# Attention heads paired j with j+6 in both batches, and the first loads cut by partition halves

## The chip, the core and the metric

The kernel runs on one core of one Trainium2 chip. The time is device microseconds of a whole execution; the number that counts is the median of several executions. The kernel before took 660.87 us (three runs: 656.98, 660.87 and 662.31). The profile shown here is of one further execution that took 657.37 us.

## The reference

Two batches of 12 heads, 448 queries and keys, 64 numbers per head, all float32. The scores of the heads are mixed before the softmax by a 12 by 12 matrix, and the probabilities are mixed again after it:

```python
scores = scale * np.matmul(q, k.transpose(0, 1, 3, 2))
scores = np.einsum('bhij,hg->bgij', scores, w_pre)
attn = softmax(scores)                       # over the last axis
attn = np.einsum('bhij,hg->bgij', attn, w_post)
x = np.matmul(attn, v)
```

The result (896 rows of 768) goes through two feed-forward pairs of layers, 768 to 2048 to 768, the first with a hard-swish and the second with a leaky unit with a learned slope. Their weights are handled as 64-bit bit patterns and rebuilt as pairs of float32 numbers, a high and a low part, so that three products of the two parts give the precision.

## The kernel before, in words

**Stages.** Attention fills roughly the first 180 us of the program, the two feed-forward layers the rest. In attention the 448 queries of a batch are cut into four tiles of 120, 120, 120 and 88 queries, so there are eight tiles. For every tile the scores of 12 heads are computed as six pairs of heads (`qk`): one head of a pair lives in partitions 0 to 63 of the key tile `kst` and the query tile `qst`, the other in partitions 64 to 127. Each pair is four matrix products of 448 columns (two blocks of queries for each head; in the profile each counts as two instructions), and its two PSUM tiles are copied to the score tile `S` by ScalarE (first head) and VectorE (second head).

**From scores to mixing.** The mixing by `w_pre` needs, for ten queries, all 12 heads on the partition axis. This is made by a DMA from SBUF to SBUF (`pull`): 120 rows of 1792 bytes, issued by SyncE, two pulls for each mixing step. A step (`premix`, `exp`, `norm`, `post`) then mixes, takes the exponential, and mixes again. `S` must hold all heads of a tile before its first pull can start.

**Order.** The program is written out by hand, and each engine executes its list in order. SyncE issues nearly all DMAs; ScalarE issues a few at the very start. The completion of a DMA is counted on one of eight semaphores that are handed out in turn, so each DMA waits, before it is issued, for the one eight places earlier in the program.

**The start.** The queries of tile 0 come in three pieces (pair 0, pairs 1 and 2, pairs 3 to 5), each cut into the two partition halves: SyncE issues the lower half and ScalarE the upper half. The keys of batch 0 come in five DMAs of all 128 partitions: pair 0 (by ScalarE), pairs 1, 2 and 3 alone, and pairs 4 and 5 together. The array `k0` in memory has the even heads in its first 64 rows and the odd heads in the other 64, so that pair j is heads 2j and 2j+1. The query array has one row for each of the 64 numbers of a head, and in it, for each tile, the 12 heads one after the other; a pair of heads 2j and 2j+1 therefore takes pieces of 120 floats (480 bytes) that lie two heads apart. The queries of tile 1 come in two pieces of two halves, with the small loads of `w_pre` and `w_post` in between, and the queries of the other tiles in two halves each. All keys of batch 1 come later, in four DMAs of one partition half and three pairs each, from rows that lie two heads apart (1792-byte pieces).

The lines that the change touches are `load_k0` (L112), `load_k` (L115), `load_q` (L132), `qk` (L163) and the list of first loads (L538 to L554). The copies of `S` are at L566, the pulls at L189, the first mixing product at L199, the second one at L238.

Of the kernel before, what the change touches and what calls it, by code (L numbers as in the profile page):

```python
# [18 lines left out]
Z = 4  # L19
# [16 lines left out]
def kernel(  # L36
# [15 lines left out]
    nc = tc.nc  # L52
    _, D, H, S = k.shape
    B, D = q.shape[0], D // 2
# [13 lines left out]
    tiles = []  # L68
    groups = []
    for b in range(B):  # L70
        for i0 in range(0, S, GP):
            n = min(GP, S - i0)
            t = len(tiles)
# [33 lines left out]
    with tc.manual_schedule():  # L107
        xT = xtp.tile([128, KD, NT], F32, name="xT")
        v_t, q_st = {}, {}
        k_st = [kq.tile([128, H // 2, S], F32, tag=f"k{b}", name="kst") for b in range(B)]  # L110

        def load_k0(p, z, q=nc.sync):  # L112
            q.dma_start(out=k_st[0][:, p:z, :], in_=k0[:, p:z, :])

        def load_k(b, o, p, z):  # L115
            src = k[b - 1, D * o:D * o + D].rearrange("p (j o) s -> p j o s", o=2)
            nc.sync.dma_start(out=k_st[b][D * o:D * o + D, p:z, :], in_=src[:, p:z, o, :])

        wraw = late.tile([128, WP], F32, tag="wraw", bufs=1, name="wraw")
        nc.gpsimd.memset(wraw, 0.0)  # L120
        wpre = late.tile([128, Q], F32, tag="wpre", bufs=1, name="wpre")
        nc.gpsimd.memset(wpre, 0.0)
        wpost = late.tile([128, WP], F32, tag="wpost", bufs=1, name="wpost")
        load_k0(0, 1, nc.scalar)
        nc.vector.memset(three, 3.0)
        nc.vector.memset(warm, 0.0)
        nc.scalar.activation(out=warm, in_=warm, func=ACTF.Exp)

        def upper(n):
            return max(n - (Q - Z), 36)  # L130

        def load_q(ti, *at, qs=(nc.sync, nc.sync)):  # L132
            T = tiles[ti]
            n = T["n"]
            m = H // 2 * n
            t = q_st[ti] = kq.tile([128, Z + H // 2 * GP], F32, tag="qst", bufs=2, name="qst")
            nc.gpsimd.memset(t[:, :Z], 0.0)
            z = Q + m - n + upper(n)
            if z > Z + m:
                nc.gpsimd.memset(t[:, Z + m:z], 0.0)  # L140
            at = (0, *at, H // 2)
            for x, y in zip(at, at[1:]):
                for o in range(2):
                    d = slice(D * o, D * o + D)
                    a = T["i0"] * H
                    src = q[T["b"], d, a:a + H * n].rearrange("p (j o n) -> p j o n", o=2, n=n)
                    qs[o].dma_start(
                        out=t[d, Z + x * n:Z + y * n].rearrange("p (j n) -> p j n", n=n),
                        in_=src[:, x:y, o, :],
                    )  # L150
                yield

# [8 lines left out]
        S_t, MT = {}, {}  # L161

        def qk(ti, j, tag="sc"):  # L163
            n = tiles[ti]["n"]
            if j == 0:
                S_t[ti] = s_pool[(NTILE - 1 - ti) % 3].tile([128, H, S], F32, tag="S", name="S")
            pool_ = psB if tag == "sc" else psA
            ps = [pool_.tile([128, 512], F32, tag=tag, bufs=2, name="sc") for _ in range(2)]
            t = q_st[ti]
            k_ = k_st[tiles[ti]["b"]]  # L170
            for o in range(2):
                b = j * n
                for a, z, r in ((b, b + Q, 0), (b + Q, b + Q + upper(n), Q)):
                    nc.tensor.matmul(  # L174
                        ps[o][r:r + z - a, :S], t[D * o:D * o + D, a:z], k_[D * o:D * o + D, j, :],
                        start=True, stop=True,
                    )
            return [(S_t[ti][:Z + n, 2 * j + o, :], ps[o][:Z + n, :S]) for o in range(2)]

        d_t, mx_t, e_t, sm_t, wr_t, pt_t = {}, {}, {}, {}, {}, {}  # L180

# [292 lines left out]
        def in_chain(i, xs, c):  # L474
            p = ptile()[:, :S]
            in_part(p, i, xs, c, 0, KD)
            return p
# [57 lines left out]
            return i  # L535


        q0 = load_q(0, 1, 3, qs=(nc.sync, nc.scalar))  # L538
        next(q0)
        load_k0(1, 2)  # L540
        next(q0)
        load_k0(2, 3)
        load_k0(3, 4)
        next(q0)
        load_k0(4, H // 2)
        for c in range(2):
            a = GH * c
            nc.sync.dma_start(out=wpre[Z + GH * c:Z + GH * c + GH, :GH], in_=w_pre[a:a + GH, a:a + GH])
        q1 = load_q(1, 3)
        next(q1)  # L550
        for c in range(2):
            a = GH * c
            nc.sync.dma_start(out=wraw[Q * c:Q * c + GH], in_=w_post[a:a + GH, a:a + GH])
        next(q1)  # L554
        for _ in range(4):
            d_buf.append(late.tile([128, 2, S], F32, tag=f"pull{len(d_buf)}", bufs=1, name="pull"))
            nc.gpsimd.memset(d_buf[-1][:Z], 0.0)
# [10 lines left out]
        for j in range(H // 2):  # L568
            s_out(qk(0, j, ("sc", "mx")[j % 2]))
# [7 lines left out]
        for i in range(NC):  # L577
            a = 2 * (14 + 8 * i)
# [26 lines left out]
        for c in range(4):  # L605
            load_at.setdefault((3, 5, 7, 8)[c], []).append(lambda c=c: load_v(0, c))
            load_at.setdefault(10 + c, []).append(
                lambda c=c: load_k(1, c % 2, 3 * (c // 2), 3 * (c // 2) + 3)
            )
            load_at.setdefault(tiles[tps]['s'] // 2 + 5 + c, []).append(lambda c=c: load_v(1, c))  # L610

        for p_ in range(-2, NP + 1):
            if p_ == -2:
                for g in range(6):
                    if g == 2:
                        list(load_q(2))
                    pull(g)
# [12 lines left out]
            if 0 <= p_ < NP:  # L630
                premix(p_)
            av_add()
            two = [lambda ti=ti, j=j: qk(ti, j, "mx" if p_ < 0 and j % 2 else "sc") for ti, j in qk_at.get(p_, [])]
            pend = [f() for f in (two if p_ < 0 else two[:1])]
            if 0 <= p_ < NP:
# [46 lines left out]
        for f in range(NC):  # L682
            p = in_chain(f, x_t, 1)
# [134 lines left out]
```

## Time and profile before

| | us |
|---|---|
| median of three runs | 660.87 |
| lowest and highest | 656.98, 662.31 |
| profiled execution, whole | 657.37 |
| its span, first to last instruction | 655.5 |
| TensorE busy in the span | 635.8 (97%) |
| start of the first mixing step | 17.09 |

The span is 1.87 us shorter than the whole execution. TensorE is the busiest engine; the granted clock was 0.997 of full speed over the span. The times in the profile's rows count from the start of the span. In the rows, a wait is written behind an instruction in square brackets with the engine or DMA that seems to have ended it; `issue` means that the profile shows no such event.

### The profile page before, as it was taken

What the parts mean: (1) busy time and instruction counts of PE and PEld (TensorE: products, weight loads), DVE (VectorE), ACT (ScalarE), POOL (GpSimd) and SP (SyncE); (2) the same over time, 40 slices, a digit from 0 to 9 for tenths busy, and PEclk for the clock granted to TensorE, in tenths of its full rate; (3) what the DMA queues carried; (4) which work ended last, traced back from release to release, by engine and by line L of the source; (5) the groups of instructions that cost most, each with busy time, mean ns of one, the idle gap of its engine ahead of it and who ended that gap; (6) DMA issues with size and microseconds to landing.
All of it is one profiled execution on the core that took longest, in us unless ns stands there. A gap on an engine that the chain in (4) does not pass through costs nothing.

```text
span 655.5 us, 17580 instructions
## 1 busy us (share of the span) xinstructions
PE 635.8 (97%) x7464; PEld 558.9 (85%) x7464; DVE 407.2 (62%) x640; ACT 354.1 (54%) x664; POOL 291.5 (44%) x236
## 2 busy tenths in 40 slices
PE   7988899999899999999999999999999999999997
PEld 2666687777689999999999999999999999999997
DVE  4754575756545778787734543489999997443401
ACT  4776788887765665666444533444444444444310
POOL 2111131323533454545577545445544555777430
PEclk9999999999899999999999999999999999999999
DMA  5778654754401332233344242213322224335202
GB/s 164 241 221 196 177 143 171 212 182 128 131 3 50 101 137 100 96 108 132 98 145 144 97 145 96 97 54 110 125 98 96 97 96 138 136 136 206 97 0 85
DMA packets 34923, 81.82 MB, mean 125 GB/s; under 512 B 11420, under 2 KB 24988, under 8 KB 34844
## 3 DMA queue, kind: packets, MB, share of 16 engines
q1 hardware_dynamic: 34268, 80.27, 37.9%
q8 instruction: 59, 0.97, 0.6%
q10 hardware_dynamic: 576, 0.41, 0.2%
q14 instruction: 20, 0.16, 0.1%
HBM read 58.65 MB, written 2.75 MB: 94 GB/s over the span
## 4 chain that ended last, share of the span: by engine, by line
PE 87%; issue 5%; POOL 4%; ACT 1%; DVE 1%; DMA 0%; POOLq 0%; DVEq 0%; ACTq 0%
PE p L466 63%; PE pt L238 6%; PE av L301 6%; PE mx L199 6%; PE sc L174 6%; POOL wb L388 2%; POOL wlo L399 2%; ACT e L214 1%; DVE nm L205 1%; DMA qst<-in_q_dram 0%; ACT MT L253 0%; ACT xh L461 0%; DVE xT L279 0%; POOL wr L226 0%; DVE o L737 0%
## 5 line engine op out<-in xcount | busy, mean ns | idle before, releaser
L399 POOL TENSOR_TENSOR wlo<-wb,whi 128x768 fp32r<-128x768 f32 x64 | 126.8, 1981 | 130.7 <-ACT whi L393 130.7
L388 POOL TENSOR_TENSOR wb<-wb,wst 128x768 int32<-128x768 int32 x64 | 125.4, 1960 | 81.6 <-DVE wb L381 64.9
L466 PE MATMUL p<-xh,whi 128*128 128x448 f32 x384 | 140.6, 366 | 0.0
L466 PE MATMUL p<-xh,wlo 128*128 128x448 f32 x384 | 139.6, 364 | 0.0
L466 PE MATMUL p<-gh,whi 128*128 128x448 f32 x384 | 139.3, 363 | 0.0
L466 PE MATMUL p<-gh,wlo 128*128 128x448 f32 x384 | 138.9, 362 | 0.1
L466 PE MATMUL p<-gl,whi 128*128 128x448 f32 x384 | 138.7, 361 | 0.0
L466 PE MATMUL p<-xl,whi 128*128 128x448 f32 x384 | 138.7, 361 | 0.0
L373 DVE TENSOR_SCALAR wb<-wb 128x768 f32<-128x768 f32 x64 | 52.1, 814 | 81.6 <-ACT wb L357 81.6
L357 ACT ACTIVATE wb<-wst 128x768 f32<-128x768 f32 x64 | 58.3, 912 | 69.7 <-DMA wst<-in_w_out_dram 53.6
L393 ACT CAST whi<-wb 128x768 fp32r<-128x768 f32 x64 | 53.2, 832 | 48.4 <-PE p L466 30.1
L205 DVE TENSOR_REDUCE nm<-mx 128x1 f32<-128x448 f32 x90 | 52.4, 619 | 42.7 <-PE mx L199 40.5
L238 PEld LDWEIGHTS pt<-wr,e 60*64 60x64 f32 (+1 forms) x2880 | 60.1, 134 | 20.9 <-issue 11.8
L466 PEld LDWEIGHTS p<-xh,wlo 128*128 128x128 f32 x384 | 72.4, 188 | 5.6
L466 PEld LDWEIGHTS p<-gh,wlo 128*128 128x128 f32 x384 | 72.0, 187 | 5.9 <-POOL wlo L399 0.4
L466 PEld LDWEIGHTS p<-xl,whi 128*128 128x128 f32 x384 | 72.1, 188 | 5.0
L466 PEld LDWEIGHTS p<-xh,whi 128*128 128x128 f32 x384 | 72.3, 188 | 4.4 <-issue 0.2
L466 PEld LDWEIGHTS p<-gh,whi 128*128 128x128 f32 x384 | 72.1, 188 | 4.5
L214 ACT ACTIVATE e<-mx,nm 128x448 f32<-128x448 f32 x90 | 56.7, 640 | 35.3 <-DVE nm L205 34.8
L466 PEld LDWEIGHTS p<-gl,whi 128*128 128x128 f32 x384 | 71.9, 187 | 4.4
L226 POOL TENSOR_SCALAR wr<-wpost,sm 128x60 f32<-128x60 f32 x74 | 25.3, 356 | 113.2 <-DVE sm L222 110.9
L381 DVE SCALAR_TENSOR_TENSOR wb<-wst,wb 128x768 uint32<-128x768 uint32 x64 | 67.5, 1055 | 1.1
(50 smaller groups left out, 799.1 us busy)
## 6 DMA issues: line engine op xcount, KB each, us to landing
wst<-in_w_out_dram SPq DMA_DIRECT2D x32, 768.0 KB
wst<-in_w_in_dram SPq DMA_DIRECT2D x27, 768.0 KB
pull<-S SPq DMA_DIRECT2D x88, 210.0 KB
wst<-in_w_in_dram SPq DMA_DIRECT2D x10, 384.0 KB
v<-in_v_dram SPq DMA_DIRECT2D x16, 168.0 KB
out_dram<-o SPq DMA_DIRECT2D x12, 224.0 KB
qst<-in_q_dram SPq DMA_DIRECT2D x8, 180.0 KB
kst<-in_k_dram SPq DMA_DIRECT2D x4, 336.0 KB
```

The costliest lines, as they stand in the source:

```text
L174: nc.tensor.matmul(ps[o][r:r + z - a, :S], t[D * o:D * o + D, a:z], k_[D * o:D * o + D, j, :], start=True, stop=True,)
L199: nc.tensor.matmul(ms[r][Q * c:Q * c + Q, :S], wpre[a:z], d[a:z, c, :], start=True, stop=True)
L205: nc.vector.tensor_reduce(nm, m[:, :S], axis=AX.X, op=ALU.max, negate=True)
L214: nc.scalar.activation(out=e, in_=ms[o][:, :S], func=ACTF.Exp, bias=nms[o], accum_out=sm[:, o:o + 1])
L238: nc.tensor.matmul(ts[c][Q * z:Q * z + m, u:u + GH], e[a:a + GH, j:j + m], wr[a:a + GH], start=True, stop=True,)
L357: nc.scalar.activation(t, s[:, :, 1].bitcast(F32), ACTF.Abs)
L373: nc.vector.tensor_scalar(t, t, W_MAX, W_MIN, ALU.min, ALU.max)
L381: nc.vector.scalar_tensor_tensor(u, st_t[i][:, :, 1], 0xC0000000, u, ALU.bitwise_and, ALU.bitwise_or)
L388: nc.gpsimd.tensor_tensor(n, n, st_t.pop(i)[:, :, 0].bitcast(I32), ALU.add)
L393: nc.scalar.copy(hi, b_t[i])
L399: nc.gpsimd.tensor_tensor(lo, b_t.pop(i), w_t[i][0].bitcast(F32), ALU.subtract)
L466: nc.tensor.matmul(p, wt[a], xt[c], start=(first and z == 0), stop=(last and z == 2))
```

## The change

Heads are now paired j with j+6, in both batches, so that the lower partition half holds heads 0 to 5 and the upper half heads 6 to 11. The pieces of a partition half then lie side by side in memory. The queries of a tile come as rows of 6 times 120 floats, 2880 bytes (2112 for the tiles of 88), one DMA for each partition half; for tile 0 the three pieces are given up. The keys of batch 1 come from rows of three heads side by side (5376 bytes). The array `k0` keeps its layout in memory (even heads in the first 64 rows), so the keys of batch 0 are loaded for each partition half apart: its first three slots get even heads and its last three odd heads. That gives the order of pairs 0 2 4 1 3 5 in batch 0, and eight DMAs of 64 partitions instead of five of 128. The scores land at the same place in `S` as before.

```diff
-        def load_k0(p, z, q=nc.sync):
-            q.dma_start(out=k_st[0][:, p:z, :], in_=k0[:, p:z, :])
+        def load_k0(m, p, z, q=nc.sync):
+            o, a = p // 3, 3 * m + p % 3
+            q.dma_start(
+                out=k_st[0][D * m:D * m + D, p:z, :], in_=k0[D * o:D * o + D, a:a + z - p, :]
+            )
 
         def load_k(b, o, p, z):
-            src = k[b - 1, D * o:D * o + D].rearrange("p (j o) s -> p j o s", o=2)
-            nc.sync.dma_start(out=k_st[b][D * o:D * o + D, p:z, :], in_=src[:, p:z, o, :])
+            a = o * (H // 2)
+            nc.sync.dma_start(
+                out=k_st[b][D * o:D * o + D, p:z, :], in_=k[b - 1, D * o:D * o + D, a + p:a + z, :]
+            )
...
-        load_k0(0, 1, nc.scalar)
+        load_k0(0, 0, 1)
+        load_k0(1, 0, 1, nc.scalar)
...
-                    a = T["i0"] * H
-                    src = q[T["b"], d, a:a + H * n].rearrange("p (j o n) -> p j o n", o=2, n=n)
+                    a = T["i0"] * H + o * m
                     qs[o].dma_start(
-                        out=t[d, Z + x * n:Z + y * n].rearrange("p (j n) -> p j n", n=n),
-                        in_=src[:, x:y, o, :],
+                        out=t[d, Z + x * n:Z + y * n], in_=q[T["b"], d, a + x * n:a + y * n]
                     )
...
+            h0 = j if tiles[ti]["b"] else (0, 2, 4, 1, 3, 5)[j]
             for o in range(2):
-                b = j * n
+                b = h0 * n
...
-            return [(S_t[ti][:Z + n, 2 * j + o, :], ps[o][:Z + n, :S]) for o in range(2)]
+            return [(S_t[ti][:Z + n, h0 + o * (H // 2), :], ps[o][:Z + n, :S]) for o in range(2)]
...
-        q0 = load_q(0, 1, 3, qs=(nc.sync, nc.scalar))
-        next(q0)
-        load_k0(1, 2)
-        next(q0)
-        load_k0(2, 3)
-        load_k0(3, 4)
-        next(q0)
-        load_k0(4, H // 2)
+        list(load_q(0, qs=(nc.sync, nc.scalar)))
+        load_k0(0, 1, 3)
+        load_k0(1, 1, 3, nc.scalar)
+        for p, z in ((3, 4), (4, 6)):
+            for m in range(2):
+                load_k0(m, p, z)
+        list(load_q(1))
         for c in range(2):
...
-        q1 = load_q(1, 3)
-        next(q1)
...
-        next(q1)
```

The DMAs that SyncE issues from the start of the program to the first two pulls were these (`qst` are queries, `kst` keys, with partitions x floats; `wpre` and `wraw` the mixing matrices):

```order
L147 DMA qst<-in_q_dram 64x120
L113 DMA kst<-in_k_dram 128x448
L147 DMA qst<-in_q_dram 64x2x120
L113 DMA kst<-in_k_dram 128x448 x2
L147 DMA qst<-in_q_dram 64x3x120
L113 DMA kst<-in_k_dram 128x896
L548 DMA wpre<-in_w_pre_dram 60x60 x2
L147 DMA qst<-in_q_dram 64x3x120 x2
L553 DMA wraw<-in_w_post_dram 60x60 x2
L147 DMA qst<-in_q_dram 64x3x120 x2
L189 DMA pull<-S 120x1x448 x2
```

And they are now, in the same stretch:

```order
L114 DMA kst<-in_k_dram 64x448
L152 DMA qst<-in_q_dram 64x720
L114 DMA kst<-in_k_dram 64x896
L114 DMA kst<-in_k_dram 64x448 x2
L114 DMA kst<-in_k_dram 64x896 x2
L152 DMA qst<-in_q_dram 64x720 x2
L552 DMA wpre<-in_w_pre_dram 60x60 x2
L555 DMA wraw<-in_w_post_dram 60x60 x2
L194 DMA pull<-S 120x1x448 x2
```

Fifteen DMAs ahead of the pulls have become thirteen. The queries of tile 1 stand now ahead of `wpre`, in two DMAs where there were four, and the keys of pairs 3 to 5 are four DMAs of half the partitions where there were two of all.

ScalarE's list at the same place was:

```order
L113 DMA kst<-in_k_dram 128x448
L127 ACT_TABLE_LOAD
L127 ACTIVATE warm<-warm 128x16
L147 DMA qst<-in_q_dram 64x120
L147 DMA qst<-in_q_dram 64x2x120
L147 DMA qst<-in_q_dram 64x3x120
L566 COPY S<-sc 124x448 x12
```

And is now:

```order
L114 DMA kst<-in_k_dram 64x448
L133 ACT_TABLE_LOAD
L133 ACTIVATE warm<-warm 128x16
L152 DMA qst<-in_q_dram 64x720
L114 DMA kst<-in_k_dram 64x896
L567 COPY S<-sc 124x448 x12
```

ScalarE issues the upper half of the queries in one DMA where it issued three, and the upper half of the keys of the first three pairs.

## Rows read from the trace of the kernel before

**Rows 1.** The page, first part: busy time, share of the span, instructions.

```profile
PE 635.8 (97%) x7464; PEld 558.9 (85%) x7464; DVE 407.2 (62%) x640; ACT 354.1 (54%) x664; POOL 291.5 (44%) x236
```

**Rows 2.** Stretches: length, engines' busy time (instructions), granted clock, DMA share, GB/s.

```profile
0.00:16.50 16.50, 12.89 (x96) 4.87 (x96) 6.90 (x13) 7.40 (x14) 4.26 (x15) 1.00 0.60 165
16.50:30.00 13.50, 13.26 (x272) 7.72 (x273) 9.61 (x24) 10.04 (x27) 2.40 (x10) 1.00 0.74 245
30.00:60.00 30.00, 26.42 (x802) 18.84 (x795) 17.35 (x42) 22.91 (x61) 4.92 (x18) 1.00 0.79 213
...
180.00:600.00 420.00, 419.95 (x2511) 391.51 (x2504) 289.44 (x367) 208.65 (x314) 228.31 (x120) 1.00 0.32 109
```

**Rows 3.** Timeline of TensorE's weight loads: start, length, instruction, idle time before.

```profile
3.58 0.31 PEld L174 LDWEIGHTS sc<-kst,qst 64*64 64x64 f32 x4 [3.58 <-issue]
...
5.80 0.33 PEld L174 LDWEIGHTS sc<-kst,qst 64*64 64x64 f32 x8 [1.22 <-DMA kst<-in_k_dram]
...
8.72 0.43 PEld L174 LDWEIGHTS sc<-kst,qst 64*64 64x64 f32 x8 [1.10 <-ACT S L566]
9.70 0.34 PEld L174 LDWEIGHTS sc<-kst,qst 64*64 64x64 f32 x8 [0.54 <-ACT S L566]
10.63 0.34 PEld L174 LDWEIGHTS sc<-kst,qst 64*64 64x64 f32 x8 [0.59 <-ACT S L566]
...
15.87 0.19 PEld L174 LDWEIGHTS sc<-kst,qst 64*64 64x64 f32 x4 [0.25 <-DVE S L566]
17.05 0.22 PEld L199 LDWEIGHTS mx<-pull,wpre 64*64 64x64 f32 x4 [0.99 <-issue]
```

**Rows 4.** Timeline of VectorE: the copy that ends tile 0's scores.

```profile
11.80 1.38 DVE L566 COPY S<-sc 124x448 f32<-124x448 f32 x2 [0.31 <-PE sc L174]
```

**Rows 5.** Timeline of SyncE's DMA issues in the first 27 us.

```profile
5.37 0.34 SPq L113 DMA_DIRECT2D kst<-in_k_dram  x1
...
12.49 1.79 SPq L189 DMA_DIRECT2D pull<-S  x2
14.40 1.34 SPq L147 DMA_DIRECT2D qst<-in_q_dram  x2
15.78 10.25 SPq L189 DMA_DIRECT2D pull<-S  x12
```

**Rows 6.** DMA issues by size, from the page: one slot of keys.

```profile
kst<-in_k_dram ACTq DMA_DIRECT2D x1, 224.0 KB
```

**Rows 7.** Stretches of particular transfers, columns as in the second group.

```profile
2.00:9.00 7.00, 5.39 (x28) 1.81 (x32) 1.25 (x2) 1.72 (x4) 2.15 (x3) 1.00 0.90 253
...
8.50:9.00 0.50, 0.50 (x8) 0.28 (x8) 0.00 (x0) 0.00 (x0) 0.00 (x0) 1.00 1.01 332
11.00:13.00 2.00, 2.00 (x24) 0.72 (x16) 1.55 (x3) 1.40 (x3) 0.41 (x2) 1.00 0.42 92
...
50.50:51.00 0.50, 0.50 (x8) 0.15 (x4) 0.47 (x1) 0.00 (x0) 0.00 (x0) 1.00 1.07 190
```

**Rows 8.** Timeline of weight loads at the second mixing step.

```profile
20.35 0.20 PEld L199 LDWEIGHTS mx<-pull,wpre 64*64 64x64 f32 x6 [0.61 <-DMA pull<-S]
```

**Rows 9.** Chain of work that ended last: its longest stalls in attention.

```profile
46.58 1.39 issue
...
69.73 1.33 issue
...
75.50 1.24 issue
...
119.93 1.29 issue
```

**Rows 10.** SyncE's issues of later queries: three of them.

```profile
44.19 1.75 SPq L147 DMA_DIRECT2D qst<-in_q_dram  x2
...
94.17 1.35 SPq L147 DMA_DIRECT2D qst<-in_q_dram  x2
...
116.69 1.34 SPq L147 DMA_DIRECT2D qst<-in_q_dram  x2
```

## The prediction

> **What bounds the kernel now.** I read the page's busy times first: TensorE is busy for 635.8 of 655.5 us [rows 1], so what can be won lies in its idle stretches. The table by stretches then shows where these are. From 180 to 600 us there are none (419.95 of 420 us), and no line of that part is touched. In attention there are some: 3.6 us between 30 and 60 us, and the first 16.5 us, where TensorE is called busy for 12.89 us but runs only 96 products [rows 2]. The weight loads tell more there than the products, whose ends are modelled. Pair 0 of tile 0 starts at 3.58 us, pair 1 at 5.80 after 1.22 us of waiting for keys, pair 3 at 8.72, pair 4 at 9.70 and pair 5 at 10.63 [rows 3]. The waits before 8.72 and 9.70 are put down to copies of S; those copies had been done, so I take them for DMA waits, of queries and of the last keys. From pair 5 of tile 0 to the last of tile 1 (15.87) six pairs take 5.24 us, 0.87 us each: the pace of the copies out of PSUM.
>
> What hangs on this start: tile 0's last copy is the first of the two VectorE copies from 11.80 us, so it ends at about 12.49 [rows 4], and there SyncE issues the first pull [rows 5]. The two pulls are issued by 14.28, and the first mixing step loads its weights at 17.05 [rows 3], 2.8 us behind. The next two pulls, at 0.85 us each in the row of twelve from 15.78 [rows 5], are issued by 17.49, and the second step waits for a pull until 20.35 [rows 8], 2.86 us behind. So the first steps stand in the shadow of the pulls, and these in that of tile 0's scores. From there on TensorE is busy, 13.26 of 13.5 us up to 30 us [rows 2]. A start that comes d earlier moves the end by d.
>
> **The change part by part.** *Bytes of tile 0.* Six slots of keys at 224 KB [rows 6] are 1.376 MB, and 128 rows of 2880 bytes of queries 0.369 MB, together 1.745 MB, the same before and after. Before, 2 to 9 us moved 7 times 253 GB/s, 1.77 MB [rows 7], so the last keys were in at about 9.0, and pair 4, which needs them, loaded its weights 0.7 us later. Pair 5 follows 0.93 us behind, and the first pull 2.79 us behind pair 4.
>
> *What pieces of 480 bytes cost.* The second half of tile 1's queries, in such pieces and alone on the queue, moved 2 times 92 GB/s, 0.184 MB, in 0.42 times 2 us of engine time, 219 GB/s when busy; the last keys, in all 128 partitions, ran at 332 GB/s [rows 7]. With rows of 2880 bytes I expect the queries to cost what keys cost, 0.57 us less of DMA time for a tile (0.369 MB at 219 against 332 GB/s). The three pieces of tile 0's queries also no longer stand among the keys of pairs 1 to 5.
>
> *What halves cost.* The trace has one clean look at a load of one partition half: the keys of batch 1, between 50.5 and 51 us, at 190 GB/s with the DMA engines busy throughout (share 1.07) [rows 7]. That is the lower bound for the new loads; 332 GB/s is the upper. The first 1.057 MB (queries and three slots of keys) have their lower half on SyncE's queue and their upper half on ScalarE's, both in flight: I take 310 GB/s, near the upper bound, 3.4 us. The other three slots, 0.688 MB, follow on SyncE's queue alone, half after half: I take the middle, 261 GB/s, 2.6 us. From 2.0 us that ends at 8.0, so pair 4 comes at 8.7, **1.0 us earlier**. At 332 GB/s throughout it ends at 7.3 (1.7 us earlier), at 190 at 11.2 (2.2 us later).
>
> The trace's 190 GB/s for one half has a rule beside it. The Trainium skill, SBUF — State Buffer, section "Door 1: The DMA port swizzle", says that DMA bandwidth goes by how many of the 16 ports the partitions reach, and that partitions 0 to 63 reach eight. By it the last three slots would run at half of 332, an estimate of 166 GB/s, and take 4.1 us, and pair 4 would come 0.5 us later than before instead of 1.0 earlier. The trace's one look agrees with the direction of the rule.
>
> *Pair 0 waits for more.* It needs now all queries and one slot of keys, 0.598 MB, at 310 GB/s until 3.9, so it starts near 4.6 instead of 3.58. With pairs 0.87 us apart, pair 4 could start at 8.1; the keys at 8.7 are later, so this costs nothing. Were the keys faster, it would cap the gain at 1.6 us.
>
> *Tile 1.* Its queries stand behind the keys on SyncE's queue, now in two DMAs: 0.369 MB at 261 GB/s, in by 9.4, usable at 10.1. Tile 1's first pair follows pair 5 (9.6) at 10.5. Cover of 0.4 us; without it the pulls would still start on time, only TensorE's last pairs before the first mixing step would slip. `wpre` and `wraw` come behind these queries; the first mixing step at 16 us is far off.
>
> *SyncE's later issues.* Tile 2's queries are issued from 14.40 for 1.34 us in a row of DMAs without a gap [rows 5], and the second step waits behind them. Below, they might cost 0.34 us each, as the cheapest key DMA does [rows 5], a gain of 0.66 us; above, nothing changes. The two loads still spread over 64 partitions as before, so I take 0. All later queries and the keys of batch 1 become shorter transfers that no instruction of TensorE is shown to wait for: 0. ScalarE issues one DMA fewer before its first copy at 5.4 us: hidden, 0.
>
> **Sum:** 657.37 us of the profiled execution less 1.0 is 656.4. That execution lies 3.5 us below the median of the three runs; less 1.0 from there is 659.9. Since a new median can fall at either, I forecast the middle, **658.0 us**.
>
> **Rivals.** *The halves win, and the start gets later.* On SyncE's queue each half is written before the other, and two loads follow in the same order; if that holds the whole of the first load near 190 GB/s, pair 4 comes up to 2.2 us later and the time is 659.6 on the profile's base, slower than before. It decides at 249 GB/s on average, where the last byte is in at 9.0 as before. For it: the 190 GB/s of one half. Against it: two halves on two queues for 60% of the bytes. Chance 17%.
>
> *The long stalls go too.* The chain has stalls of 1.39, 1.33 and 1.29 us at 46.58, 69.73 and 119.93 [rows 9] with no releaser in the profile, the first and the third 2.4 and 3.2 us behind the start of an issue of queries [rows 10]. If crowding by 480-byte pieces makes such stalls, I would have all three go: 4.0 us more, 652.4. Against it: a stall of 1.24 us at 75.50 has no such load beside it, and the load at 94.17 no such stall [rows 9, 10]. Chance 12%.
>
> *The start is shifted and nothing comes of it*: the keys arrive at the old time, since SyncE must still issue seven loads for them and tile 0's queries one after the other, as before, at 0.34 us or more each [rows 5]. Then 657.4 on the profile's base. Chance 14%.
>
> **How the numbers follow.** Forecast 57%, rivals 17, 12 and 14. About 1% is what a measurement of this kernel can tell from no change: 6.6 us, and its own runs spread over 5.3. The bounds of the likeliest case are 1.7 us of gain under the lowest run (655.3) and 0.3 under the highest (662); the second rival reaches down to 652.4, the first up to 664.5 from the highest run. I take **653.5 to 662**, which leaves about half of each rival outside. Faster by over 1% needs the second rival and a low run, or stalls gone that I do not see: 10%. Slower by over 1% needs the first rival at its worst and a high run: 4%. Within 1%: 86%.
>
> **What would show it.** In the profile after, the weight loads of tile 0: pair 0 near 4.6 us, pair 4 near 8.7 and pair 5 near 9.6, the first pull near 11.5, the first mixing step near 16.1. The DMA rate between 2 and 8 us should be near 290 GB/s; below 249 the first rival is right. If pair 4 is at 8.7 and the mixing step still at 17, the chain from scores to pulls is not what I say. If the stalls by the query loads have gone, the second rival is. I should be wrong altogether if the feed-forward part changed its length, since nothing there is touched.

## The result and the profile after

The changed kernel took 663.0 us (median of 20 executions, 657.47 to 669.57) against 659.89 us for the kernel before beside it (20 executions, 652.69 to 664.95): a ratio of **1.0051**, 95% interval 1.0027 to 1.0076. It is slower by half a per cent, where the forecast was 658.0 us and a range of 653.5 to 662. The profiled execution took 658.5 us, span 656.7, granted clock 0.996. The ratios in this document compare fast executions only (none over 1.5% above the fastest of its kernel) and are therefore not the quotients of the medians; the differences at equal clock below use all executions and change by 0.2 us at most without the slow ones.

First the timeline of TensorE's weight loads in the changed kernel (start, length, instruction, idle time before), the answer to [rows 3, 8].

```profile
6.77 0.44 PEld L179 LDWEIGHTS sc<-kst,qst 64*64 64x64 f32 x8 [6.77 <-issue]
8.03 0.68 PEld L179 LDWEIGHTS sc<-kst,qst 64*64 64x64 f32 x8 [0.82 <-DMA kst<-in_k_dram]
9.18 0.41 PEld L179 LDWEIGHTS sc<-kst,qst 64*64 64x64 f32 x4 [0.47 <-ACT S L567]
...
10.67 0.41 PEld L179 LDWEIGHTS sc<-kst,qst 64*64 64x64 f32 x8 [0.52 <-ACT S L567]
11.48 0.35 PEld L179 LDWEIGHTS sc<-kst,qst 64*64 64x64 f32 x8 [0.40 <-ACT S L567]
...
18.70 0.22 PEld L204 LDWEIGHTS mx<-pull,wpre 64*64 64x64 f32 x4 [0.83 <-issue]
...
21.83 0.22 PEld L204 LDWEIGHTS mx<-pull,wpre 64*64 64x64 f32 x6 [0.47 <-DMA pull<-S]
```

Pair 0 starts at 6.77 us (before 3.58, forecast 4.6) and pair 4 at 11.48 (before 9.70, forecast 8.7). The first mixing step is at 18.70 (before 17.05, forecast 16.1). It is 1.65 us late, and the second step still 1.48.

The chain of waits (start, length, what) says what pair 0 waited for. In the changed kernel:

```profile
0.74 0.59 SPq L114
...
1.38 5.29 DMA qst<-in_q_dram
...
6.80 11.84 PE sc L179 x94
...
198.72 302.42 PE p L471 x1511
```

The same view of the kernel before:

```profile
0.74 2.73 DMA qst<-in_q_dram
...
3.61 13.23 PE sc L174 x90
...
197.91 302.42 PE p L466 x1511
```

The queries are issued at 1.38 us and counted as landed 5.29 us later; before, the small first piece was there after 2.73 us. The lower lines are the longest unbroken run of feed-forward products: 302.42 us in both, so that part kept its length, as the prediction said it must. It starts 0.81 us later, so in these two executions about half of the 1.65 us at the first step is left there.

Two more views of the changed kernel: SyncE's queue (start, length, what), the answer to [rows 5],

```profile
0.74 0.59 SPq L114 DMA_DIRECT2D kst<-in_k_dram  x1
1.38 0.82 SPq L152 DMA_DIRECT2D qst<-in_q_dram  x1
2.25 3.17 SPq L114 DMA_DIRECT2D kst<-in_k_dram  x5
...
14.30 1.80 SPq L194 DMA_DIRECT2D pull<-S  x2
```

and the stretches, columns as in [rows 2, 7]:

```profile
2.00:4.50 2.50, 0.00 (x0) 0.00 (x0) 0.00 (x0) 0.82 (x2) 2.15 (x3) 1.00 0.87 220
4.50:9.00 4.50, 2.19 (x12) 1.02 (x16) 0.27 (x1) 0.41 (x1) 0.00 (x0) 1.00 1.01 287
2.00:9.00 7.00, 2.19 (x12) 1.02 (x16) 0.27 (x1) 1.23 (x3) 2.15 (x3) 1.00 0.96 263
16.50:30.00 13.50, 13.42 (x278) 7.35 (x273) 10.08 (x22) 9.74 (x25) 1.89 (x8) 1.00 0.69 247
30.00:60.00 30.00, 27.15 (x791) 20.23 (x786) 16.82 (x41) 22.11 (x58) 4.85 (x17) 0.94 0.69 208
```

The first pull is issued 2.82 us behind pair 4 and the first mixing step 4.40 us behind the first pull, near the forecast's 2.8 and 4.6. So the chain from scores to pulls is as described; its start is late. From 2 to 9 us the DMA engines moved 263 GB/s, more than before (253) and above the 249 at which the first rival decides. Its first 2.5 us had only 220 GB/s, where 310 was forecast; the kernel before had 226 there. From 16.5 to 30 us TensorE is busy 13.42 of 13.5 us (13.26 before), so nothing there takes the late start back. From 30 to 60 us it is busy longer than before (27.15 against 26.42) for fewer products, at a granted clock of 0.94 instead of 1.00. The kernel before has such a stretch too, 0.94 between 150 and 180 us, so this need not be the change's doing (see the last section).

Last, the score products of the changed kernel by duration (count; minimum, median, maximum in ns; first and last start), the long ones first and then the short ones, without the few of a length between:

```profile
L179 PE MATMUL sc<-kst,qst x16: 947/951/999, 6.8 to 9.2; 64*64 64x448 f32 x8, 64*60 64x448 f32 x8
...
L179 PE MATMUL sc<-kst,qst x58: 536/537/588, 10.3 to 16.0; 64*64 64x448 f32 x29, 64*60 64x448 f32 x29
```

The same of the kernel before:

```profile
L174 PE MATMUL sc<-kst,qst x24: 947/951/1006, 3.6 to 8.1; 64*64 64x448 f32 x12, 64*60 64x448 f32 x12
...
L174 PE MATMUL sc<-kst,qst x66: 536/537/587, 9.5 to 15.9; 64*64 64x448 f32 x33, 64*60 64x448 f32 x33
```

One and the same product takes 951 ns at first and 537 later. The kernel before passes to the short products at 9.5 us, the changed one at 10.3. Before, half of tile 0's 48 products were long, while the keys were still coming; now a third are, but all of them fall behind the arrival of the queries. The prediction saw none of this: it took 0.87 us a pair throughout.

### The profile page after: what moved, and what is told of

Read it like the earlier page. It is cut to its first block, busy times and chain, and to the rows that moved or that the text cites. A ratio compares the mean times of both kernels' runs of the same rounds, so it can differ in the third digit from the quotient of the medians.

```text
span 656.7 us, 17575 instructions
## 1 busy us (share of the span) xinstructions
PE 633.6 (96%) x7464; PEld 557.2 (85%) x7464; DVE 412.5 (63%) x640; ACT 355.0 (54%) x664; POOL 290.3 (44%) x236
## 4 chain that ended last, share of the span: by engine, by line
PE 86%; issue 5%; POOL 4%; ACT 2%; DVE 1%; DMA 1%; SPq 0%; POOLq 0%; ACTq 0%; DVEq 0%
PE p L471 63%; PE pt L243 6%; PE av L306 6%; PE mx L204 6%; PE sc L179 5%; POOL wb L393 2%; POOL wlo L404 2%; ACT e L219 1%; DMA qst<-in_q_dram 1%; DVE nm L210 1%; ACT MT L258 0%; DVE xT L284 0%; POOL wr L231 0%; ACT S L567 0%; ACT wst L368 0%
## 5 line engine op out<-in xcount | busy, mean ns | idle before, releaser
L404 POOL TENSOR_TENSOR wlo<-wb,whi 128x768 fp32r<-128x768 f32 x64 | 125.2, 1956 | 129.3 <-ACT whi L398 129.3
L243 PEld LDWEIGHTS pt<-wr,e 60*64 60x64 f32 (+1 forms) x2880 | 59.0, 134 | 24.3 <-issue 15.8
L386 DVE SCALAR_TENSOR_TENSOR wb<-wst,wb 128x768 uint32<-128x768 uint32 x64 | 72.4, 1130 | 1.1
```

What stands on the lines that cost most here:

```text
L243: nc.tensor.matmul(ts[c][Q * z:Q * z + m, u:u + GH], e[a:a + GH, j:j + m], wr[a:a + GH], start=True, stop=True,)
L386: nc.vector.scalar_tensor_tensor(u, st_t[i][:, :, 1], 0xC0000000, u, ALU.bitwise_and, ALU.bitwise_or)
L404: nc.gpsimd.tensor_tensor(lo, b_t.pop(i), w_t[i][0].bitcast(F32), ALU.subtract)
```

## The experiments

**How the times compare.** The executions of any kernel here spread over some 10 us, and the mean granted clock of an execution (0.987 to 1.000) goes with its time and explains about half of the spread. A line fitted through the 98 executions of the kernel before and 33 of the changed one, gathered over all comparisons, has a slope of -620 us per unit of clock, 0.6 us for each 0.001. "At equal clock" below is the difference to those 98 after this correction, with its standard error; the printed ratio has no such correction. The slow first products are not part of that clock (see the last section), so the correction leaves them in.

**When a load is in.** The trace also keeps when each of the 16 DMA engines reported its share of a load. The times of "the last engine" below are read from there; the first instruction that waits for a load starts right behind its last engine (pair 0 of the changed kernel at 6.77 us, 0.10 behind the last report of its queries).

**e1: the queries uncut, nothing else.** The kernel before, with tile 0's queries as one load of two halves (still in 480-byte pieces):

```diff
-        q0 = load_q(0, 1, 3, qs=(nc.sync, nc.scalar))
-        next(q0)
+        list(load_q(0, qs=(nc.sync, nc.scalar)))
...
```

> The kernel before with one edit: the queries of tile 0 come in one DMA for each partition half (six 480-byte pieces a row) instead of three pieces. Theory 1 (pair 0 now waits for all queries of tile 0, and that is what delays the start): pair 0's weight load moves from 3.58 us to 5.0 or later, the first mixing step from 17.05 to 17.8 to 18.7, and the time is 0.5 to 1.7 us longer. Theory 2 (the key loads of one partition half are what delays it): all loads of keys are of 128 partitions here, so pairs 1 to 5 and the first mixing step stay where they were (within 0.3 us of 17.05) although pair 0 starts later.

Measured: 664.12 against 660.23 us, ratio 1.0055 (1.0018 to 1.0093); at equal clock +2.9 ± 0.6 us. Weight loads of this kernel:

```profile
4.59 0.30 PEld L174 LDWEIGHTS sc<-kst,qst 64*64 64x64 f32 x4 [4.59 <-POOL pull L554]
7.75 0.30 PEld L174 LDWEIGHTS sc<-kst,qst 64*64 64x64 f32 x8 [2.85 <-DMA qst<-in_q_dram]
...
20.15 0.19 PEld L199 LDWEIGHTS mx<-pull,wpre 64*64 64x64 f32 x2 [0.55 <-issue]
```

The second half of pair 0 waits 2.85 us for queries, and the mixing step is 3.1 us later than before: the direction of theory 1, but well beyond its 17.8 to 18.7 us and its 0.5 to 1.7 us of time. Giving up the pieces is alone enough to make the kernel slower, and with 480-byte pieces it costs more than in the changed kernel.

**e2: the keys whole.** The changed kernel, with the keys of batch 0 laid out in memory by heads 0 to 5 and 6 to 11, so that they come in five DMAs of 128 partitions and the order of pairs is 0 to 5 again:

```diff
+        def load_k0(p, z, q=nc.sync):
+            q.dma_start(out=k_st[0][:, p:z, :], in_=k0[:, p:z, :])
...
-            h0 = j if tiles[ti]["b"] else (0, 2, 4, 1, 3, 5)[j]
+            h0 = j
...
```

> The changed kernel with the keys of batch 0 in 128 partitions again, in five DMAs (one slot, 1, 1, 1, 2) as before: the key array is laid out with heads 0 to 5 in its first 64 rows, so the pairs come in the order 0 to 5. Queries still whole, in 2880-byte rows. Theory 1 (waiting for all queries of tile 0): pair 0 still starts at 6.0 us or later and the first mixing step stays at 18.2 or later. Theory 2 (halves of keys): pair 0 starts at 4.6 to 5.2 and the first mixing step comes at 16.5 or earlier.

Measured: 659.59 us, ratio 0.9988 (0.9963 to 1.0013); at equal clock -0.8 ± 0.4 us. Weight loads:

```profile
4.54 0.31 PEld L175 LDWEIGHTS sc<-kst,qst 64*64 64x64 f32 x4 [4.54 <-POOL pull L553]
5.59 1.03 PEld L175 LDWEIGHTS sc<-kst,qst 64*64 64x64 f32 x10 [0.75 <-DMA qst<-in_q_dram]
...
17.84 0.22 PEld L200 LDWEIGHTS mx<-pull,wpre 64*64 64x64 f32 x4 [0.66 <-issue]
```

and the stretch from 2 to 9 us:

```profile
2.00:9.00 7.00, 4.43 (x22) 2.38 (x26) 0.73 (x2) 1.71 (x4) 2.15 (x3) 1.00 1.00 302
```

Here 302 GB/s and a pair 0 at 4.54: about what the prediction assumed for the changed kernel. And yet the mixing step is at 17.84, not near 16. Neither theory's numbers hold as written: the start is earlier than the one said, the step later than the other said. Something beyond the arrival sets the step. Nor is the shape of the keys' loads all that differs: SyncE now issues its half of the queries first, at 0.74 us instead of 1.38, so 0.64 of the 2.2 us that pair 0 gains on the changed kernel may be that.

**e3: the pairing alone.** e2 with tile 0's queries in the old three pieces and tile 1's in the old two:

```diff
-        list(load_q(0, qs=(nc.sync, nc.scalar)))
+        q0 = load_q(0, 1, 3, qs=(nc.sync, nc.scalar))
+        next(q0)
...
```

> As the run with keys of 128 partitions, and the queries of tiles 0 and 1 cut into the pieces that they had before, in the order of before: so the kernel before with heads paired j with j+6 and all pieces of a row side by side, and nothing else. Both theories: pair 0 starts near 3.6 us again. If rows without gaps help as I forecast, the keys of pairs 4 and 5 come earlier (0.5 us or so, since queries no longer take 219 GB/s), the first mixing step at 16.2 to 16.8, and the time is 0.3 to 1 us shorter than before; if the rest of the changed kernel's loss lies in the later loads of queries and of batch 1's keys, the time is 1 us or more longer than before although the start is early.

Measured: 659.76 us, ratio 0.9988 (0.9953 to 1.0022); at equal clock -2.1 ± 0.5 us, the largest gain of all kernels by this measure, which its ratio does not show apart from no change. Weight loads:

```profile
3.65 0.31 PEld L175 LDWEIGHTS sc<-kst,qst 64*64 64x64 f32 x4 [3.65 <-issue]
...
6.42 0.33 PEld L175 LDWEIGHTS sc<-kst,qst 64*64 64x64 f32 x8 [1.66 <-DMA kst<-in_k_dram]
...
18.01 0.22 PEld L200 LDWEIGHTS mx<-pull,wpre 64*64 64x64 f32 x4 [0.99 <-issue]
```

The step at 18.01 misses the 16.2 to 16.8 expected. Pair 1 starts only at 6.42 us. The row puts its wait down to keys, but the last engine reported these at 5.46 us and the queries of pairs 1 and 2 at 6.32, so it waited for queries. The short products begin at 10.8 us.

**e4: the changed kernel with a first piece of queries for pair 0.**

```diff
-        list(load_q(0, qs=(nc.sync, nc.scalar)))
+        list(load_q(0, 1, qs=(nc.sync, nc.scalar)))
```

> The changed kernel with the queries of tile 0 in two pieces (pair 0 alone, then the other five) in place of one; keys in halves as in the change. Theory 1: pair 0 starts at 4.0 to 4.6 us instead of 6.77, pair 1 still waits for its queries and keys until 7.5 to 8.3, and since the copies of pair 0 are then long done the later pairs follow at 0.85 us each: first mixing step at 17.2 to 18.0 instead of 18.70. Theory 2 (the keys' halves set the pace): the first mixing step stays at 18.4 or later.

Measured: 661.11 us, ratio 1.0004 (0.9974 to 1.0034). Weight loads:

```profile
4.88 0.44 PEld L179 LDWEIGHTS sc<-kst,qst 64*64 64x64 f32 x8 [4.88 <-POOL pull L558]
7.99 0.47 PEld L179 LDWEIGHTS sc<-kst,qst 64*64 64x64 f32 x8 [2.66 <-issue]
8.79 0.41 PEld L179 LDWEIGHTS sc<-kst,qst 64*64 64x64 f32 x4 [0.33 <-issue]
...
10.39 0.43 PEld L179 LDWEIGHTS sc<-kst,qst 64*64 64x64 f32 x4 [0.44 <-ACT S L567]
...
11.88 0.43 PEld L179 LDWEIGHTS sc<-kst,qst 64*64 64x64 f32 x4 [0.44 <-ACT S L567]
...
20.35 0.22 PEld L204 LDWEIGHTS mx<-pull,wpre 64*64 64x64 f32 x4 [1.10 <-issue]
```

and its products between 9 and 14 us:

```profile
L179 PE MATMUL sc<-kst,qst x33: 537/951/999, 8.0 to 14.0; 64*60 64x448 f32 x17, 64*64 64x448 f32 x16
```

Pair 0 comes 1.9 us earlier than in the changed kernel, and the mixing step 1.65 us later, at 20.35 where 17.2 to 18.0 was expected. After pair 0 TensorE stood 2.66 us; the short products began only at 13.9 us, and the pairs from 8.79 on stand 1.5 us apart instead of 0.87. An early pair followed by a gap bought nothing. This miss made the pace of the products the next thing to test.

**r_e4, r_before, r_after: second profiles of the same kernels.**

> The changed kernel with the first pair's queries in a piece of their own, a second profile. Its first profile had pair 0 at 4.88 us, long products until 14 us and the first mixing step at 20.35, later than the changed kernel's own, while its measured time was no longer than that of the kernel before. If the gap of 2.7 us between pairs 0 and 1 keeps TensorE slow, the long products last until 12 us or later again and the mixing step comes at 19 us or later; if that profile was a stray one, the mixing step comes at 17.2 to 18.5.

> The kernel before once more, for a second profile of it. If the first mixing step of one profile is worth comparing, it comes at 17.05 us within 0.4 us here too; if the landing of the first loads or the length of the first products differs from run to run, it can lie up to 2 us away.

> The changed kernel once more, for a second profile. Theory 1 (pair 0 waits for all queries and three DMAs' worth of keys): its weight load comes again at 6.0 to 7.5 us, against 3.6 before, and the first mixing step at 18.3 to 20.5. If that first profile was a stray one: pair 0 near 4.6.

Measured: r_e4 has pair 1 at 7.88 behind a gap of 2.36 us, short products from 13.9 us on and the step at 20.34, so e4's profile was no stray. r_before has the step at 17.63, a little outside the 0.4 us expected, and r_after at 19.29: 1.66 us apart, beside 1.65 in the first two profiles.

**w_before, w_after, w_e2: TensorE kept at work before pair 0.** Products of a zeroed piece of `S`, 224 columns each, in a PSUM tile that nothing else uses at that time: three ahead of pair 0 and one ahead of pair 1 in the kernel before, seven ahead of pair 0 in the changed one, five in e2.

```diff
+        S_t[0] = s_pool[(NTILE - 1) % 3].tile([128, H, S], F32, tag="S", name="S")
+        nc.vector.memset(S_t[0][:, H - 1, :224], 0.0)
...
+        dummy = psA.tile([128, 512], F32, tag="pt", bufs=2, name="dummy")
+
+        def busy(n):
+            for _ in range(n):
+                nc.tensor.matmul(dummy[:, :224], S_t[0][:, H - 1, :128], S_t[0][:, H - 1, :224], start=True, stop=True)
...
+            busy((5, 0)[j] if j < 2 else 0)
```

> The kernel before with four products of zeros on TensorE (128 x 224), three ahead of pair 0 and one ahead of pair 1; their results are not used. In the profile before, the products of the first pairs took 951 ns each until about 8.1 us and 537 ns after that. Theory A (they are long because TensorE had been idle): the long ones end 1.5 to 2.5 us earlier, the first mixing step comes at 15.8 to 16.8, and the time falls by 0.3 to 1.2 us. Theory B (they are long because of where their data comes from, or the queue behind them): they stay long until 8 us and the first mixing step stays near 17.05 or comes later by up to 1 us.

> The changed kernel with seven such products of zeros ahead of pair 0, which waits for its data until 6.77 us anyway. Theory A: the products of tile 0 take 537 ns from pair 0 on, pairs 1 to 5 follow at 0.85 us from 8.0, the first mixing step comes at 17.0 to 17.8 instead of 18.70, and the time falls by 0.9 to 1.7 us against the changed kernel, which leaves it 0.2 to 0.4% above the kernel before. Theory B: no change in the first mixing step (18.4 or later).

> Heads paired j with j+6, keys of batch 0 in five DMAs of 128 partitions, queries in whole rows of 2880 bytes, and five products of zeros ahead of pair 0: the version that the runs so far point to. If the start is set by the landing of the loads once TensorE is warm: pair 0 at 4.6 to 5.8 us as without the zeros, products of 537 ns from pair 0 or 1 on, the later pairs at 0.8 us, pair 4 near 8.8, first mixing step at 15.8 to 16.6 against 17.84 without the zeros, and the time 0.2 to 0.5% below the kernel before. If the first mixing step is held by something else (pulls, queries of tile 1): 17 us or later, and no gain over the run without zeros.

Measured for w_after: 659.76 us, ratio 0.9982 (0.9951 to 1.0013); at equal clock 0.0 ± 0.5 us. Weight loads:

```profile
6.28 0.22 PEld L181 LDWEIGHTS sc<-kst,qst 64*64 64x64 f32 x8 [0.28 <-issue]
7.57 0.20 PEld L181 LDWEIGHTS sc<-kst,qst 64*64 64x64 f32 x8 [1.08 <-DMA kst<-in_k_dram]
...
9.93 0.34 PEld L181 LDWEIGHTS sc<-kst,qst 64*64 64x64 f32 x8 [0.41 <-ACT S L569]
...
17.20 0.19 PEld L206 LDWEIGHTS mx<-pull,wpre 64*64 64x64 f32 x2 [0.90 <-issue]
18.84 0.30 PEld L206 LDWEIGHTS mx<-pull,wpre 64*64 64x64 f32 x6 [1.46 <-DMA pull<-S]
```

and its products up to 9 us:

```profile
L181 PE MATMUL sc<-kst,qst x24: 536/536/587, 6.3 to 8.8; 64*64 64x448 f32 x12, 64*60 64x448 f32 x12
```

With work ahead of them the score products take 536 ns from the first. From pair 0 to pair 4 it is now 3.65 us instead of 4.71, and the step comes at 17.20 instead of 18.70. Of these 1.5 us some 0.5 are pair 0's own earlier start, which varies as much from one execution of the changed kernel to another (below). Beside r2_after, whose pair 0 starts alike (6.21) and whose step is at 18.25, 1.05 us remain for the pace.

w_before: 658.74 us, ratio 0.9974 (0.9938 to 1.0010), step at 17.48 where 15.8 to 16.8 was expected. Its products are short from 5.2 us on, but pairs 3 and 4 load at 8.54 and 10.25, after 1.32 and 1.37 us of waiting; the last engines reported pair 3's queries at 8.48 and pair 4's keys at 10.15. So in the kernel before, the loads hid the slow products almost wholly, and short ones are worth little there.

w_e2: 658.34 against 661.22 us, ratio **0.9948** (0.9912 to 0.9984); at equal clock -1.6 ± 0.7 us. Weight loads:

```profile
5.21 0.29 PEld L177 LDWEIGHTS sc<-kst,qst 64*64 64x64 f32 x4 [0.54 <-issue]
...
9.35 0.26 PEld L177 LDWEIGHTS sc<-kst,qst 64*64 64x64 f32 x8 [0.69 <-ACT S L564]
...
16.57 0.22 PEld L202 LDWEIGHTS mx<-pull,wpre 64*64 64x64 f32 x4 [1.11 <-issue]
```

This is the earliest first mixing step of all kernels, 1.27 us ahead of e2 and as expected, and the only kernel whose interval lies below 1: by this one comparison of twelve executions it beats the kernel before, and its median is lower than either of the changed kernel's two (663.0 and 661.38), which come from other comparisons.

**d_late: the new pairing in batch 1 only.** The kernel before, with the new `load_k`, `load_q` and `qk` where `T["b"]` is 1.

> The kernel before with the new pairing in batch 1 alone: the keys of batch 1 in 5376-byte pieces and the queries of its four tiles in 2880-byte rows (2112 for the small one), batch 0 and all first loads as before. If the changed kernel's loss lies in its start alone: the ratio is 1.000 within 0.0025. If part of it lies in the later loads: a ratio of 1.002 or more, 1.3 us, which is about what the start's 1.65 us leave unexplained of the changed kernel's 0.51%.

Measured: 660.54 us, ratio 0.9988 (0.9953 to 1.0023); at equal clock +0.1 ± 0.4 us. The shorter transfers of batch 1 cost nothing, and no gain of them can be told. This profile also has the start of the kernel before with short products from 7.4 us on instead of 9.5, and its first mixing step is at 17.27: there again the earlier short products gain nothing, and pair 4 (10.04) follows its keys (9.94).

**x_keys_sp: the upper keys of pairs 1 and 2 on SyncE.** The changed kernel with these keys issued by SyncE instead of ScalarE, so that they no longer run beside the queries on ScalarE's queue:

```diff
-        load_k0(1, 1, 3, nc.scalar)
+        load_k0(1, 1, 3)
```

> The changed kernel with the upper half of the keys of pairs 1 and 2 issued by SyncE, behind the lower half, instead of ScalarE: nothing but queries then follows the first keys on ScalarE's queue. If the queries of tile 0 land late because those keys run beside them on the other queue: pair 0 starts at 5.3 to 6.1 us instead of 6.77 to 6.90. If it is the queries' own transfer that is slow: 6.5 us or later as before.

Measured (one execution): 661.37 us; the stretch from 2 to 4.5 us has 249 GB/s, and pair 0, at 6.32, lies within what the changed kernel itself gave (6.21 to 6.90 in three profiles). That the keys crowd the queries out is not shown by pair 0. The trace shows it in part: fourteen of the 16 DMA engines reported the upper half of the queries by 4.75 us (5.44, 5.75 and 5.55 in the changed kernel), but the last one, which decides, at 5.98 (6.22, 6.51 and 5.86).

**r2_after: the changed kernel timed again.**

> The changed kernel once more, timed beside the kernel before, with the granted clock of every execution on both sides. If the start's 1.65 us is all that the change costs: at equal granted clock (0.6 us for each 0.001, from the slope of its first 20 executions) it is 1.2 to 2.1 us slower than before, and what is left of the first 0.51% is a lower mean clock in that set. If the change costs more than its start: 2.8 us or more at equal clock.

Measured: 661.38 against 660.67 us, ratio 1.0029 (0.9996 to 1.0063); the profile has pair 0 at 6.21 and the step at 18.25. Over all executions with a listed clock the changed kernel's mean is 662.46 us (33) and that of the kernel before 660.99 (98), 1.5 us apart; at equal clock 1.1 ± 0.4 us. So the change costs about 0.2%, near the shift at the first mixing step, and the first comparison's 0.5% lies above that. What is left fits the spread between sets of executions: the kernel before had 659.89 us there, 660.23 to 661.52 in the four later comparisons.

## Why the prediction was wrong

**The step that failed** is "*Pair 0 waits for more*", with its conclusion that "the keys at 8.7 are later, so this costs nothing". With it failed the term that brought the last keys in at 8.0 us. Three numbers were wrong.

*When pair 0 starts.* The prediction worked out the arrival as bytes by rate, 0.598 MB at 310 GB/s. From 2 to 4.5 us the rate was 220 GB/s, and the queries were counted as landed at 6.67 us, 5.29 us after the issue, when at 266 GB/s from 2 us on over 1.2 MB had come in. So queries and first keys did not come first: the loads issued behind them came in beside them. Fourteen of the 16 DMA engines had reported the lower half of the queries by 5.78 us, the last did at 6.67; by then fourteen had reported the upper keys of pairs 1 and 2 as well, which were issued 0.6 us later. A load counted as landed here with its slowest engine, which a sum of bytes by rate leaves out. The row that could have warned was the kernel before's own: its first piece took 2.73 us, though small. e1 shows the same without any change to the keys' halves (second half of pair 0 at 7.75).

*When the last keys are in.* The sum had 8.0 us; the last engine reported them at 10.10, and at 9.59 in the kernel before, where the prediction had 9.0. In other executions it was 10.49 and 10.10 in the changed kernel and 10.30 in the kernel before, so the halves brought the keys no earlier, and the 1.0 us of the sum was not there to be won. With whole keys (e2) it was 8.83.

*How fast the pairs follow.* The 0.87 us came from rows between 10.63 and 15.87 us. While the products take 951 ns, a pair takes 1.5 us. From pair 0 to pair 4 the changed kernel takes 4.71 us where 3.5 stood in the sum, and 3.65 with the zero products ahead (w_after). By the sum's own arithmetic, 6.77 plus 3.5 gives 10.25 for pair 4; two of the pairs at 1.5 us make it 11.5, and 11.48 was measured. Pair 1's key wait of 0.82 us adds nothing: its weights are loaded while the products of pair 0 still run, and its own products start at 8.32 us, in the step of about 0.75 us that all the long ones keep. In the prediction the keys set pair 4; in the run pair 4 followed the pairs ahead of it, 1.4 us behind its keys. Rows with 951 ns were in the trace of before, and the prediction set them aside because the ends of products are modelled. Their starts say the same: 5.83, 7.35 and 8.84 us for pairs 1 to 3 of the kernel before.

**Readings of single rows.** The waits before 8.72 and 9.70 us in the kernel before were for queries and keys, as the prediction took them: the last engines reported at 8.66 and 9.59. Pair 1's wait until 5.80 was for queries (5.70), not for keys (5.35), though the row names these.

**What held.** From pair 4 to the first pull 2.82 us (2.8), from there to the mixing step 4.40 (4.6), and the feed-forward part untouched. The time stayed within 1%, to which the prediction gave 86%, but not for the reason given: the start it had 1.0 us earlier came 1.65 us later. The later loads cost nothing (d_late). Tile 1's queries stop no pair ahead of the pulls.

**"A start that comes d earlier moves the end by d"** holds only roughly: +1.65 us at the step is 1.1 ± 0.4 at the end, and e1's +3.1 is 2.9 ± 0.6, but e4's +3.3 is 1.0 ± 0.6, and e3, whose step is 0.4 to 1.0 late, is 2.1 faster. What makes up for it in e3 and e4 stays open. Both have batch 0's queries of the later tiles in long rows, but so has the changed kernel.

**The rivals.** *The halves win* had the right sign, but not the mechanism: it decides at 249 GB/s and 263 were moved, and pair 4, 1.8 us later than before, did not wait for its keys. In part it was right all the same: with whole keys (e2) the same stretch has 302 GB/s and pair 0 comes 2.2 us earlier, though up to 0.64 us of that is the earlier issue of the queries. The rule set beside it, from the Trainium skill, SBUF — State Buffer, section "Door 1: The DMA port swizzle", would have given 166 GB/s for the last three slots; from 7.1 to 9 us, when SyncE's queue alone moved data, one half behind another, 259 were measured, so that estimate does not hold here. The Trainium skill, DMA: Bandwidth & Descriptors, section "Rules for kernel authors", advises one transfer of all partitions instead of two of disjoint halves; 302 against 263 GB/s agrees with that.

*The long stalls go too* is not borne out. The chain of the changed kernel still has them, in other places:

```profile
48.25 2.31 issue
...
70.70 1.01 issue
...
125.81 1.27 issue
```

Together 4.59 us, beside 1.39, 1.33, 1.24 and 1.29 before [rows 9], 5.25 in all. Nor do places or sum belong to a kernel: a second execution of the kernel before (r_before) has 2.54, 1.05, 1.16 and 2.13 us at 66.72, 135.15, 139.90 and 175.49.

*The start is shifted and nothing comes of it* had the keys right, at about their old time (10.10 us, beside 9.59 and 10.30 before), but left the start where it was; it moved, and later.

**Still open:** why one or two DMA engines report the queries so much later than the others, and what starts the long stalls and the stretches at the lower clock, which differ from one execution of a kernel to another.

## What to carry to other kernels

At the start of a program, take the landing time of a load from the row of a like load, not from bytes by rate: what is issued behind it comes in beside it, and it counts as landed with its slowest engine. A small first load is no cure by itself: in e4 it made pair 0 1.9 us earlier and the first mixing step 1.65 us later. Look at the durations of the same instruction in the first microseconds and later before taking one pace for both; a wait for data can hide slow products, and a later arrival then pays for them. For a difference of a few tenths of a per cent, list the granted clock of each execution beside its time before explaining the rest.

## What was not expected of the hardware

The score products took 951 ns at first and 536 later while the granted clock in the table of stretches read 1.00 (the upper level, 2.4 GHz) in both [rows 2]; that column does not show this. The clock record kept with the trace says why: it begins only at 9.31 us in the kernel before and at 10.05 in the changed one, at the upper level, and the table counts time without a record as full. In all fifteen kept profiles the record begins within 0.2 us of the first short products, between 5.1 and 13.9 us. Which level held before that is not on record; 951 against 536 is a factor of 1.8, near the 2 between the levels of 2.4 and 1.2 GHz.

TensorE had done nothing before the slow products. With zero products ahead the score products took 536 ns from the first (w_after), and with a gap of 2.66 us behind pair 0 the short ones began at 13.9 us instead of 10.3 (e4). The moment also differs from one execution to another: 9.5, 9.9 and 7.4 us in three with the start of the kernel before (before, r_before, d_late), 10.3, 11.3 and 9.4 in the changed kernel. The Trainium skill, TensorE: Matmul & The Clock Gate, section "Part 1: The HAM clock gate", says that a TensorE which has stood idle starts at half its clock; the durations agree in direction.

The mean granted clock of whole executions ran from 0.987 to 1.000 for one kernel and another, 0.6 us for each 0.001. In the kept traces that mean is made by stretches at the lower level (1.2 GHz), which come at other places in each execution: at 173 us in the kernel before, at 20 and 177 in r_before, and at 51, 73 and 177 in the three of the changed kernel, there each behind the longest stall of TensorE (from 48.25, 69.90 and 173.38 us). Traces without one (e2, w_before) have a mean of 1.000. The three kernels with zero products had higher means (0.9966 to 0.9976) than the kernel before in the same comparisons (0.9950 to 0.9952), but e4 without them had 0.9967; whether one causes the other was not tried.
